# The second expert layer's output product as seven block products, with its gate and value stage run over the tokens in two passes

## The chip, the cores and the metric

The kernel runs on one core of a Trainium2 chip. The metric is the time on the device in microseconds (us), as the median of three runs. Engines are named as the profile names them: PE is TensorE (PEld its weight loads, LDWEIGHTS), DVE is VectorE, ACT is ScalarE, POOL is GpSimd, SP is SyncE, whose queue issues the DMAs.

## The reference, cut to what matters

```python
x = attention(q, k, v, s)                    # 2304 tokens x 512
x = moe_ref(rms_norm(x), w_gate, w_val, w_out)      # first expert layer
def moe2_ref(x, w_gate, w_val, w_out):       # second expert layer
    g = x @ w_gate                           # 512 -> 1536
    silu = g * (1.0 / (1.0 + np.exp(-g)))
    val = x @ w_val                          # 512 -> 1536
    return silu * val @ w_out                # 1536 -> 512, the product changed here
```

Inputs are float32, the expert weights float64 (8 bytes an element).

## The kernel before

**An order made by a planner.** The program records every operation with its engine, its assumed duration, what it reads and writes, and a priority (`op`, L95). `Plan.run` (L130) then makes a list schedule: at each step the engine that is free first takes the ready operation with the smallest priority number. The result is one fixed order for each engine and for SP's DMA queue; on the chip each engine works through its list in that order and waits by semaphores. Operations with several engines in a list (`[(POOL, ...), (DVE, ...)]`) go to the one that is free. The assumed durations (`c_mm`, `c_tt` and the like) are the planner's own numbers and not those of a trace.

**Three matmuls for one.** Every operand of the large products is split in a high part H and a low part L (both fp32r): H by a copy on ACT, L by a subtraction on DVE or POOL. A product is then W_H x_H + W_H x_L + W_L x_H, three matmuls into one PSUM bank, and each of them has its own LDWEIGHTS of 128x128.

**Stages.** Attention and the first gate and value stage (`moe1`, L937) share PE until 537 us. Then follow, with names used below:

1. the first output layer (`out_layer`, L1154, with `out_mm`, L1128): hidden h (1536 rows, 12 blocks f of 128) times `w_o`, for five groups of tokens (`TGROUPS`: four of 512, one of 256). Each block of h is read back from DRAM (`h_d`) into a ring of two buffers, split, and multiplied: 4 output blocks x 3 matmuls for one f.
2. the second gate and value stage: for each of 12 blocks f of the weights `w2_gv`, `load_w2` (L1177) reads the float64 values, converts them, makes the Strassen sums and splits them; then `pair_unit` (L1256) does 42 matmuls of 512 columns on token groups 0 and 1 together (seven block products instead of eight), `plain_unit` (L1316) 24 matmuls of 256 columns on group 4, and `pair_unit` again 42 on groups 2 and 3. Results go to DRAM (`h2_d`).
3. the second output layer: the same `out_layer` with `w2_o` (loop at L1392), 12 matmuls for each f and group, evacuated by `out_store` (L1137) and written to the output.

```python
for i, (w, x) in enumerate(((0, 0), (0, 1), (1, 0))):     # L1131
    op(PE, c_mm(n), lambda en, ...: en.matmul(
        acc_[d]()[:, :n], Wo[w]()[:, c], HL[x](), ...
```

PSUM is eight banks: four `mo` (shared by whoever comes), `sps0`, `sps1`, `tp0`, `tp1`. SBUF is divided in pools that are opened and closed in turn: `m1` (first gate and value stage) must be closed, when its last user is done, before `m2` can be opened (`swap_m1`, L1093).

Of the kernel before, what the change touches and what calls it, by code (L numbers as in the profile page):

```python
# [69 lines left out]
def whole(x):  # L70
    return x if isinstance(x, Part) else (x, None)


class Plan:
# [16 lines left out]
    def __init__(self):  # L91
        self.ops = []
        self.live = {}

    def op(self, eng, ns, fn, r=(), w=(), pri=0.0, later=0, port=False):  # L95
# [13 lines left out]
        for accesses, writes in ((r, False), (w, True)):  # L109
            for a in accesses:  # L110
                buf, part = a if isinstance(a, tuple) else (a, None)
                key = buf if isinstance(buf, str) else buf.key
                live = self.live.setdefault(key, [])
# [181 lines left out]
def tile_kernel(  # L295
# [729 lines left out]
    def later_buf(pool, tag, shape, dtype, name=None):  # L1025
        b = buf(pool, tag, shape, dtype, name)
        if b.key not in plan.live:
            plan.live[b.key] = list(plan.live[pool])
        return b

    def obuf(tag, shape, dtype, name=None):
        return later_buf("o", tag, shape, dtype, name)

    def m2buf(tag, shape, dtype, name=None):
        return later_buf("m2", tag, shape, dtype, name)

    def claim(*bufs):

        for b in bufs:
            op(NONE, 0, lambda en: None, w=[b])  # L1040

    raws = [obuf(f"cvs{i}", [P, 2 * DM], I32) for i in range(2)]
    cvy_o = obuf("cvy", [P, 512], F32)

    def load_o(src, f, HL, pri):

        H, L = HL
        stage = raws[f % 2]
        sub = [(POOL, c_ptt(DM)), (DVE, c_tt(DM))]
        value = load_raw(src[f * P:(f + 1) * P, :], stage, pri)  # L1050
        op(ACT, c_act(DM) + 35, lambda en: en.activation(H(), value(), ACTF.Copy),
           r=[stage], w=[H], pri=pri)
        op(sub, 0, lambda en: en.tensor_tensor(out=L(), in0=value(), in1=f32(H()),
                                               op=ALU.subtract),
           r=[stage, H], w=[L], pri=pri, port=True)

    def load_raw(src, stage, pri):

        n = src.shape[-1]
        if src.dtype == F32:  # L1060
            op(SP, 4 * P * n, lambda en: en.dma_start(out=stage().bitcast(F32)[:, :n], in_=src),
               w=[stage], pri=pri)
            return lambda: stage().bitcast(F32)[:, :n]

        def value(dtype=F32):
            return stage().bitcast(dtype).rearrange("p (n w) -> p n w", w=2)[:, :, 0]
# [4 lines left out]
            cvy_o().bitcast(F16).rearrange("p (n w) -> p n w", w=2)[:, :, 1],  # L1071
            stage().bitcast(BF16).rearrange("p (n w) -> p n w", w=4)[:, :, 2], ACTF.Copy),
           r=[stage], w=[cvy_o], pri=pri)
        op(DVE, c_tt(n), lambda en: en.scalar_tensor_tensor(  # L1074
            out=value(U32), in0=value(U32), scalar=13, in1=cvy_o().bitcast(U32),
            op0=ALU.logical_shift_right, op1=ALU.bitwise_or), r=[stage, cvy_o], w=[stage],
           pri=pri, port=True)
        return value

    def out_places(f):  # L1080
        return tuple(obuf(f"o{z}{f}", [P, DM], F32R) for z in "HL")

    clear([cvy_o], -900)
    W1o = []
    for f in range(KF):
        W1o.append(out_places(f))
        load_o(w_o, f, W1o[f], P_ATT + 1000 + f)
# [8 lines left out]
    op(NONE, 0, swap_m1, w=m1_keys + ["m2"])  # L1096

    P2 = 1.0e5
    hturn = {}
    hdeep = {"h": ["hh0", "hh1"], "H": ["hH0", "hH1"], "L": ["hL0", "hL1"]}  # L1100
    halves = {}

    def hring(z, dtype, n):

        k = hturn[z] = hturn.get(z, -1) + 1
        tags = hdeep[z]
        if n > 256:
# [28 lines left out]

    def out_store(acc_, n, tiles, pri, dst=None, key=None, any_engine=False):  # L1137
        for d in range(KD):
            xo = tiles[d]
            op([(ACT, c_act(n)), (DVE, c_tt(n))] if any_engine else ACT, c_act(n), {  # L1140
                ACT: lambda en, d=d, xo=xo: en.activation(
                    xo(), acc_[d]()[:, :n], ACTF.Copy, scale=0.5),
                DVE: lambda en, d=d, xo=xo: en.tensor_scalar(
                    out=xo(), in0=acc_[d]()[:, :n], scalar1=0.5, scalar2=None,
                    op0=ALU.mult)}, r=[acc_[d]], w=[xo], pri=pri)
            if dst is not None:
                op(SP, 4 * P * n, lambda en, d=d, xo=xo: en.dma_start(out=dst(d), in_=xo()),
                   r=[xo], w=[(key, d)], pri=pri)

    def banks(odd):  # L1150
        return [mo_bank() for _ in range(4)] if odd else \
            [bank(t) for t in ("sps0", "sps1", "tp0", "tp1")]

    def out_layer(gi, h_dram, key, Wo, pri, odd, by_row=False):  # L1154

        n = TGROUPS[gi][1]
        a = banks(odd)
        for f in range(KF):
            hh = hring("h", F32, n)
            op(SP, 4 * P * n, lambda en, hh=hh, f=f: en.dma_start(out=hh(), in_=h_dram[gi][f]),  # L1160
               r=[(key, f) if by_row else key], w=[hh], pri=pri + f)
            out_mm(a, Wo[f], split_h(hh, n, -1.0e4), f, n, pri + f)
        return a

    NPAIR = 2
    A_ROWS = {"A11": 0, "A12": 1, "A21": 2, "A22": 3, "S1": 4, "S2": 5, "S3": 6, "S4": 7}
    B_ROWS = ("B11", "B21", "B22", "T1", "T2", "T3", "T4")
    sums = m2buf("sf", [P, 1024], F32)  # L1170
    w2_tags = [("w2H", "w2L"), ("x1g0", "x1g1")]
    def wide_buf(tag, shape, dtype, name):
        b = m2buf(tag, shape, dtype, name)
        claim(b)
        return b

    def load_w2(f, pri):  # L1177

        H, L = (wide_buf(w2_tags[f % 2][z], [P, 2048], F32R, f"w2{'HL'[z]}") for z in range(2))
        gate, val = (load_raw(w2_gv[f, :, 512 * z:512 * z + 512], raws[z], pri)  # L1180
                     for z in range(2))
        g1, g2, v1, v2 = (lambda t=t, c=c: t()[:, c:c + 256]
                          for t in (gate, val) for c in (0, 256))

        def S(i):
            return sums()[:, 256 * i:256 * i + 256]
        two = [(POOL, c_ptt(256)), (DVE, c_tt(256))]
        for i, (a, b, sign, r) in enumerate((
                (v1, v2, ALU.add, raws[1:]), (lambda: S(0), g1, ALU.subtract, [(sums, 0), raws[0]]),
                (g1, v1, ALU.subtract, raws), (g2, lambda: S(1), ALU.subtract, [(sums, 1), raws[0]]))):  # L1190
# [252 lines left out]
```

## Time and profile before

| | |
|---|---|
| three runs | 1097.58, 1098.05, 1099.43 us (median 1098.05) |
| the profiled execution's own time | 1097.84 us |
| its span, first to last instruction | 1096.1 us |
| PE busy | 1078.8 us (98%), 6580 matmuls |
| DVE, ACT, POOL busy | 675.9, 583.5, 208.1 us |
| DMA | 131.42 MB, mean 120 GB/s |

The span is what the profiler saw of one execution, 1.74 us less than that execution's own time. Busy time of PE is the time in which at least one matmul was in flight; a matmul of 512 columns lasts 0.39 us from its start to its end but the next one starts 0.23 us after it, so prices of matmuls are distances between starts. Idle time of an engine that is not the bottleneck costs nothing.

### The profile page before, as it was taken

What the parts mean: (1) busy time and instruction counts of PE and PEld (TensorE: products, weight loads), DVE (VectorE), ACT (ScalarE), POOL (GpSimd) and SP (SyncE); (2) the same over time, 40 slices, a digit from 0 to 9 for tenths busy, and PEclk for the clock granted to TensorE, in tenths of its full rate; (3) what the DMA queues carried; (4) which work ended last, traced back from release to release, by engine and by line L of the source; (5) the groups of instructions that cost most, each with busy time, mean ns of one, the idle gap of its engine ahead of it and who ended that gap; (6) DMA issues with size and microseconds to landing.
All of it is one profiled execution on the core that took longest, in us unless ns stands there. A gap on an engine that the chain in (4) does not pass through costs nothing.

```text
span 1096.1 us, 19019 instructions
## 1 busy us (share of the span) xinstructions
PE 1078.8 (98%) x6580; PEld 973.5 (89%) x6580; DVE 675.9 (62%) x1755; ACT 583.5 (53%) x1266; POOL 208.1 (19%) x300
## 2 busy tenths in 40 slices
PE   7899999999999999999999999999999999999998
PEld 5599999999999999999978889888888888888888
DVE  7798788796787766652344437676677566632222
ACT  5877777766775764531244336544554455543222
POOL 4344444423333220210000000121122111000000
PEclk9999999999999999999999999999999999999999
DMA  5974444333332213641233333232232223654342
GB/s 159 301 257 136 112 122 126 117 114 94 98 108 75 80 41 121 182 137 47 70 121 96 99 97 93 91 113 85 101 139 101 88 92 129 210 180 132 99 135 96
DMA packets 81616, 131.42 MB, mean 120 GB/s; under 512 B 12848, under 2 KB 42544, under 8 KB 81520
## 3 DMA queue, kind: packets, MB, share of 16 engines
q1 hardware_dynamic: 81520, 130.20, 37.9%
q8 instruction: 52, 0.85, 0.3%
q14 instruction: 44, 0.36, 0.1%
HBM read 97.05 MB, written 33.10 MB: 119 GB/s over the span
## 4 chain that ended last, share of the span: by engine, by line
PE 84%; DMA 3%; DVE 2%; ACT 1%; issue 1%; POOLq 0%; POOL 0%; ACTq 0%; DVEq 0%; SPq 0%
PE mo L921 23%; PE mo L1132 12%; PE mo L1274 10%; PE sps L1274 8%; PE tp L1132 6%; PE sps L1132 6%; PE tp L708 4%; PE tp L692 4%; PE sps L628 4%; PE mo L1325 3%; DMA cvs<-in_w_o 2%; PE tp L1274 1%; PE mo L828 1%; ACT cvy L1070 1%; DVE cvs L1074 0%
## 5 line engine op out<-in xcount | busy, mean ns | idle before, releaser
L921 PE MATMUL mo<-xH,H 128*128 128x320 f32 (+1 forms) x768 | 228.0, 297 | 0.8 <-DVE x L905 0.8
L921 PE MATMUL mo<-xL,H 128*128 128x320 f32 (+1 forms) x768 | 227.8, 297 | 0.0
L921 PE MATMUL mo<-xH,L 128*128 128x320 f32 (+1 forms) x768 | 227.7, 297 | 0.0
L921 PEld LDWEIGHTS mo<-xH,H 128*128 128x128 f32 x768 | 144.1, 188 | 1.9 <-DVE x L905 1.0
L921 PEld LDWEIGHTS mo<-xL,H 128*128 128x128 f32 x768 | 144.3, 188 | 0.7 <-issue 0.2
L921 PEld LDWEIGHTS mo<-xH,L 128*128 128x128 f32 x768 | 144.3, 188 | 0.4
L665 ACT ACTIVATE sc<-sc,col 128x512 f32<-128x512 f32 (+4 forms) x160 | 96.0, 601 | 64.3 <-DVE col L654 63.7
L1120 DVE TENSOR_TENSOR hL<-hh,hH 128x512 fp32r<-128x512 f32 (+1 forms) x90 | 58.2, 651 | 114.8 <-ACT hH L1117 114.6
L1117 ACT ACTIVATE hH<-hh 128x512 fp32r<-128x512 f32 (+1 forms) x90 | 52.5, 587 | 114.9 <-PE mo L1132 55.9
L928 ACT ACTIVATE t<-mo 128x256 f32<-128x256 f32 (+1 forms) x108 | 43.1, 399 | 58.5 <-PE mo L921 57.9
L930 DVE SCALAR_TENSOR_TENSOR t<-t,mo 128x256 f32<-128x256 f32 (+1 forms) x108 | 48.1, 445 | 40.4 <-ACT t L928 39.4
L692 PE MATMUL tp<-ident,sc 128*128 128x128 f32 x432 | 65.5, 276 | 0.0
L700 DVE TENSOR_TENSOR pTB<-tp,pTB 128x512 fp32r<-128x512 f32 (+1 forms) x96 | 54.4, 575 | 14.5 <-ACT pTB L697 12.4
L933 DVE TENSOR_TENSOR hh<-t,mo 128x256 f32<-128x256 f32 (+1 forms) x108 | 48.0, 445 | 18.9 <-PE mo L921 18.0
L1280 ACT ACTIVATE u<-sps 128x512 f32<-128x512 f32 x48 | 28.7, 598 | 54.1 <-PE sps L1274 54.0
L1132 PE MATMUL mo<-hL,oH 128*128 128x512 f32 (+1 forms) x144 | 54.4, 378 | 0.0
L628 PE MATMUL sps<-kHH,qst 128*128 128x288 f32 (+4 forms) x160 | 54.2, 346 | 0.0
L1132 PE MATMUL mo<-hH,oH 128*128 128x512 f32 (+1 forms) x144 | 54.0, 377 | 0.0
L1132 PE MATMUL mo<-hH,oL 128*128 128x512 f32 (+1 forms) x144 | 53.8, 377 | 0.0
L1289 ACT ACTIVATE u<-u 128x512 f32<-128x512 f32 x48 | 29.7, 633 | 43.7 <-DVE u L1284 43.7
L654 DVE CUSTOM_DVE_ANT_0 sc<-sps,cb 128x384 f32<-128x384 f32 (+3 forms) x112 | 48.9, 443 | 6.4 <-PE sps L628 5.3
L697 ACT ACTIVATE pTB<-tp 128x512 fp32r<-128x512 f32 (+1 forms) x96 | 47.0, 502 | 10.9 <-PE tp L692 5.9
(221 smaller groups left out, 2795.3 us busy)
## 6 DMA issues: line engine op xcount, KB each, us to landing
hh<-h_d SPq DMA_DIRECT2D x72, 256.0 KB, 2.6
cvs<-in_w_gv SPq DMA_DIRECT2D x28, 511.8 KB, 4.6
h_d<-u SPq DMA_DIRECT2D x48, 256.0 KB, 2.0
cvs<-in_w_o SPq DMA_DIRECT2D x24, 511.8 KB, 4.0
h_d<-hh SPq DMA_DIRECT2D x84, 128.0 KB, 1.9
raw<-in_w_gv SPq DMA_DIRECT2D x20, 511.8 KB, 5.7
lq<-in_qk SPq DMA_DIRECT2D x32, 288.0 KB, 3.6
cb<-cum_d SPq DMA_DIRECT2D x32, 288.0 KB, 3.5
```

The costliest lines, as they stand in the source:

```text
L628: op(PE, c_mm(n), lambda en, pt=pt, o=o, c=c, n=n, z=z, kk=kk: en.matmul(pt()[:, :n], qst[j]()[:, o:o + 128], kk()[:, c:c + n], start=z == ...
L654: op(DVE, c_tt(w), lambda en: en.tensor_tensor_reduce(out=sc()[:m, c:c + w], in0=pt()[:m, c - at:c - at + w], in1=bias()[:m, c + off:c + o ...
L665: op(ACT, c_act(o + m, 2) + 35, lambda en: en.activation(sc()[:m, :o + m], sc()[:m, :o + m], ACTF.Exp, scale=-1.0, bias=col()[:m, 0, t:t + 1],
L692: op(PE, C_TR, lambda en, pt=pt, a=a, m=m, kb=kb, t=t: en.transpose(pt()[:, a:a + P], self.sc[t]()[:, kb * P:kb * P + P], ident()), r=[sel ...
L700: op(DVE, c_tt(n), lambda en, pt=pt, a=a, d0=d0, n=n, kn=kn: en.tensor_tensor(out=L()[:kn, d0:d0 + n], in0=pt()[:kn, a:a + n], in1=f32(H() ...
L921: op(PE, c_mm(n), lambda en, a=a, x=x, c=c, k=k, i=i: en.matmul(ps()[:, :n], a()[:, c], x()[:, k, :n], start=(k == 0 and i == 0), stop=(k ...
L930: op(DVE, c_tt(n), lambda en: en.scalar_tensor_tensor(out=t()[:, :n], in0=t()[:, :n], scalar=1.0, in1=gp()[:, :n], op0=ALU.add, op1=ALU.mu ...
L933: op(DVE, c_tt(n), lambda en: en.tensor_tensor(out=hh()[:, :n], in0=t()[:, :n], in1=vp_()[:, :n], op=ALU.mult), r=[vp_, t], w=[hh], pri=pri)
L1117: op(ACT, c_act(n) + 35, lambda en: en.activation(H(), src(), ACTF.Copy), r=[src], w=[H], pri=pri)
L1120: lambda en: en.tensor_tensor(out=L(), in0=src(), in1=f32(H()), op=ALU.subtract),
L1132: op(PE, c_mm(n), lambda en, d=d, c=c, w=w, x=x, i=i: en.matmul(acc_[d]()[:, :n], Wo[w]()[:, c], HL[x](), start=(f == 0 and i == 0), stop= ...
L1274: op(PE, c_mm(n), lambda en, w=w, xx=xx, cut=cut, kk=kk, i=i: en.matmul(ps()[:, :n], W[w]()[:, cut], xx(), start=first and kk == 0 and i == 0,
```

## The change

The second output layer is written as Strassen's scheme in Winograd's form with seven products instead of eight: the weight matrix is cut in blocks A11, A12, A21, A22 of 768x256, the tokens of a group in two halves, and sums of blocks S1 to S4 are multiplied instead. A matmul then has half the columns: 256 for the four groups of 512 tokens, 128 for the group of 256. One product is 2 output blocks m x 6 blocks kk x 3 matmuls; a group takes 7 x 36 = 252.

The rest makes room and order for that. All large SBUF tiles come from two lists of slots: 36 of kind D (two rows of 512 for H and L) and 31 of kind S (one row of 512); `mem` takes the slot that has been free longest, `give` returns it. `store_w2` and `store_wo` convert the float64 weights early, form the sums once and write them to DRAM as float32 (`w2_d`, `wo_d`); `reload_w2` and `fetch_wo` read and split them. The gate and value stage runs over the tokens twice (pass 1: groups 0 and 1; pass 2: groups 2, 3 and 4), and reads and splits `w2_d` in each pass. `first_rows` and `other_rows` read h2 and make the sums of its blocks. In the first output layer four buffers (`ahead`) are taken from pool `o`; the rest, and the weights of f = 6 to 11, need slots of `m2`.

The core of the diff (the accessors for parts of tiles, `Both`, `block`, `side`, and changes of the kind obuf to `single()` are left out):

```diff
+    lows = [single() for _ in range(2)]
+    def load_value(src, out, pri, y=lows[0]):
...
+        stage = mem("D", [P, 2 * n], I32)
...
+        give(stage)
...
+    def store_w2(f, pri):
+        V, _ = values(w2_gv[f, :, :512], w2_gv[f, :, 512:], ("A11", "A12", "A21", "A22"), pri)
+        for i in range(4):
+            X = block(V[i], (0, 1), 0, 512)
+            op(SP, 4 * P * 512, lambda en, i=i, X=X: en.dma_start(
+                out=w2_d[f, :, 512 * i:512 * i + 512], in_=X()), r=[X], w=[("w2_d", (f, i))],
+               pri=pri + 1)
+        give(*V)
+    EARLY = 6
+    W1o = [load_o(w_o, f, P_ATT + 1000 + f) for f in range(EARLY)]
+    ahead = [(pair(), single()) for _ in range(4)]
+    for f in range(KF):
+        store_w2(f, 1.0e5 + 30 + 25 * f)
+    for kk in range(KH):
+        store_wo(w2_o, wo_d, "wo_d", kk, 1.0e5 + 330 + 20 * kk)
...
+    slots("D", "w", [f"{z}{f}" for f in range(KF) for z in "HL"])
+    slots("S", "m2", [f"s{i}" for i in range(20)], "m2")
+    W1o += [load_o(w_o, f, P2 - 20 + f) for f in range(EARLY, KF)]
...
+    def reload_w2(f, pri):
+        out = []
+        for i in range(4):
+            b, t = pair(), single()
+            H, L = side(b, 0), side(b, 1)
+            dma(t, w2_d[f, :, 512 * i:512 * i + 512], 512, [("w2_d", (f, i))], pri)
+            split(t, H, L, 512, pri)
+            give(t)
+            out.append((H, L))
+        return out
...
+    def first_rows(h, key, p, at):
...
+            rows(h, key, kk, p, whole, pri)
+            combine(T[1], T[1], T[0], n, ALU.subtract, pri)
+            split(whole, side(b, 0, 0, 2, n), side(b, 1, 0, 2, n), 2 * n, pri)
...
+    def other_rows(h, key, p, at):
...
+            rows(h, key, kk + KH, p, other, pri)
+            rows(h, key, kk, p, whole, pri)
+            b21, b22 = V
+            combine(T[1], b22, T[1], n, ALU.subtract, pri)
+            combine(T[0], T[1], T[0], n, ALU.add, pri)
+            split(whole, *B, 2 * n, pri)
+            split(other, *C, 2 * n, pri)
+            combine(b21, b21, T[0], n, ALU.subtract, pri)
+            split(b21, *Ds, n, pri)
...
+    def strassen_out(h, key, W, pri, sink, G1, others):
...
+            def product(ps, a, G, i2, first, n=n):
+                for m in range(2):
+                    for kk in range(KH):
+                        HL = G[kk][1][i2]
+                        for i, (w, z) in enumerate(((0, 0), (0, 1), (1, 0))):
...
+            product(b, "A11", G1, 0, True)
+            product(c, "S1", G1, 1, True)
+            product(b, "S2", G2, 0, False)
+            product(b, "S3", G2, 1, False)
+            product(c, "S4", G3, 1, False)
+            product(c, "A12", G3, 0, True)
+            product(b, "A22", G4, 0, False)
...
     for f in range(KF):
         if f + 1 < KF:
-            W2.append(load_w2(f + 1, P3 + 40 * f - 20))
-        pair_unit(f, W2[f], X2[0], (0, 1), P3 + 40 * f)
-        plain_unit(f, W2[f], rest, 2 * NPAIR, 256, P3 + 40 * f + 10)
-        pair_unit(f, W2[f], X2[1], (2, 3), P3 + 40 * f + 20)
+            W2.append(reload_w2(f + 1, P3 + 20 * f - 10))
...
+        pair_unit(f, W2[f], X2, (0, 1), P3 + 20 * f)
+        give(*[HL[0] for HL in W2[f]])
...
+    for f in range(KF):
+        if f + 1 < KF:
+            W2.append(reload_w2(f + 1, P4 + 40 * f - 20))
...
+        pair_unit(f, W2[KF + f], X3, (2, 3), P4 + 40 * f)
+        plain_unit(f, W2[KF + f], rest, 4, 256, P4 + 40 * f + 20)
...
-    for gi, (t0, n) in enumerate(TGROUPS):
-        a = out_layer(gi, h2_d, f"h2_d{gi}", W2o, P4 + 100 * gi, gi % 2 == 0, True)
...
+    G1 = first_rows(h2_d, "h2_d", 0, P5 - 50)
+    others = other_rows(h2_d, "h2_d", 0, P5 - 45)
+    for kk in range(KH):
+        for i in (4, 6):
+            W2o[kk].update(fetch_wo(wo_d, "wo_d", kk, i, P5 - 30 + i))
+    strassen_out(h2_d, "h2_d", W2o, P5, store, G1, others)
```

**Where the order moves.** First place: PE's list for the last group of tokens (256 of them) in the second output layer. A name is the tile with its buffer number; the form at the end is the output's. Before, from the middle of the group:

```order
L1132 MATMUL mo0_11977<-hH0_11944,oH_10835 128x256
L1132 MATMUL mo0_11977<-hL0_11949,oH_10835 128x256
L1132 MATMUL mo0_11977<-hH0_11944,oL_10842 128x256
L1132 MATMUL mo2_11985<-hH0_11944,oH_10835 128x256
L1132 MATMUL mo2_11985<-hL0_11949,oH_10835 128x256
L1132 MATMUL mo2_11985<-hH0_11944,oL_10842 128x256
```

And with the change, the first of its fourteen runs of 18 matmuls (x3 is the three matmuls of one block kk, which read one tile for H and L):

```order
L1460 MATMUL mo1_13426<-H9_13126,H8_10221 128x128 x3
L1460 MATMUL mo1_13426<-L9_13131,H11_10312 128x128 x3
L1460 MATMUL mo1_13426<-H10_13137,d6_10432 128x128 x3
L1460 MATMUL mo1_13426<-L10_13143,H7_10527 128x128 x3
L1460 MATMUL mo1_13426<-d1_13151,L4_10808 128x128 x3
L1460 MATMUL mo1_13426<-d3_13163,H6_10863 128x128 x3
```

The group goes from 144 matmuls of 256 columns to 252 of 128, and the four groups of 512 tokens from 576 of 512 to 1008 of 256; all other matmuls keep their number and form.

Second place: DVE's list with the change at the seam between `moe1` and the first output layer. `hh1` is the last hidden block of `moe1`; L1112 converts float64 values, of `w_o` where it reads `L0` to `L2`; `H6_7826` is the L part of h's block f = 4, the first that does not lie in an `ahead` buffer:

```order
L949 TENSOR_TENSOR hh1_7727<-t1_7707,mo0_7703 128x320
...
L1112 SCALAR_TENSOR_TENSOR s0_7784<-L0_7291,s1_6358 128x512
L1124 TENSOR_TENSOR H0_7792<-s0_7784,H0_7792 128x512
L1112 SCALAR_TENSOR_TENSOR s1_7806<-L1_7333,s1_6358 128x512
L1112 SCALAR_TENSOR_TENSOR s4_7813<-d11_7762,s0_6352 128x512
L1129 TENSOR_TENSOR s5_7823<-s4_7813 128x256
L1124 TENSOR_TENSOR H1_7816<-s1_7806,H1_7816 128x512
L1112 SCALAR_TENSOR_TENSOR s2_7830<-L2_7374,s1_6358 128x512
L1124 TENSOR_TENSOR H6_7826<-s6_7787,H6_7826 128x512
```

Eight operations on DVE (from `s0_7784`, the first slot of `m2` that is written) now stand between the closing of `m1` and the first h block that needs it; before, both h's ring and all of `w_o` lay in pool `o`, and nothing here waited for `m1`.

Third place: DVE's list with the change at the seam between pass 2 and the second output layer. The first row is the last evacuation of pass 2 (it reads `sps0_11474`, the bank of the last matmuls); L1129 makes sums of h2's blocks, L1124 the L parts; `L1_11790` and `d2_11808` are the last two tiles that the third product, S2, reads:

```order
L1328 TENSOR_TENSOR s4_11643<-s4_11643,sps0_11474 128x512
L1129 TENSOR_TENSOR s2_11398<-s2_11398,s17_11270 128x256
L1129 TENSOR_TENSOR s5_11428<-s5_11428,s12_11453 128x256
L1129 TENSOR_TENSOR s9_11390<-s9_11390,s8_11349 128x256
...
L1129 TENSOR_TENSOR s2_11596<-s2_11596 128x256
L1124 TENSOR_TENSOR L1_11790<-s9_11588,L1_11790 128x512
L1124 TENSOR_TENSOR s10_11803<-s13_11544,s10_11803 128x256
L1124 TENSOR_TENSOR d2_11808<-s2_11596,d2_11808 128x512
```

From the row behind the evacuation to `d2_11808` it is fourteen operations, twelve of 256 columns and two of 512; PE has the products A11 and S1 (72 matmuls) and the first five blocks of S2 (15) to do meanwhile. Before, nothing but the split of single h2 blocks stood there.

## Rows read from the trace of the kernel before

**Rows 1.** The page: busy time by engine, and the granted clock in 40 slices.

```profile
PE 1078.8 (98%) x6580; PEld 973.5 (89%) x6580; DVE 675.9 (62%) x1755; ACT 583.5 (53%) x1266; POOL 208.1 (19%) x300
...
PEclk9999999999999999999999999999999999999999
```

**Rows 2.** Stretches: us, then busy us (instructions) of PE, PEld, DVE, ACT, POOL; clock, DMA share, GB/s.

```profile
466.00:560.00 94.00, 93.00 (x626) 88.75 (x627) 37.88 (x78) 23.88 (x47) 3.79 (x3) 1.00 0.30 94
560.00:663.00 103.00, 103.00 (x456) 85.14 (x455) 43.47 (x68) 40.97 (x73) 0.00 (x0) 1.00 0.33 98
663.00:957.00 294.00, 294.00 (x1500) 251.80 (x1498) 197.81 (x307) 153.86 (x273) 46.94 (x42) 1.00 0.33 113
957.00:1075.00 118.00, 117.87 (x518) 96.71 (x517) 34.93 (x52) 39.95 (x66) 0.00 (x0) 1.00 0.42 133
```

**Rows 3.** The chain that ended last, 1000 to 1097 us: start us, us, what.

```profile
1010.01 32.64 PE mo L1132 x144
...
1075.29 16.21 PE mo L1132 x135
1091.52 1.50 DVE oo L1143 x4
```

**Rows 4.** PE's timeline, two matmuls of 128 columns between longer ones: start us, us, what.

```profile
253.91 0.22 PE L628 MATMUL sps<-kHH,qst 128*128 128x128 f32 x1
253.97 0.27 PE L628 MATMUL sps<-kLL,qst 128*128 128x128 f32 x1
254.08 0.36 PE L921 MATMUL mo<-xL,H 128*128 128x320 f32 x1
```

**Rows 5.** PEld's timeline, the weight loads at the same place.

```profile
253.91 0.19 PEld L628 LDWEIGHTS sps<-kLL,qst 128*128 128x128 f32 x1
254.02 0.19 PEld L921 LDWEIGHTS mo<-xL,H 128*128 128x128 f32 x1
254.13 0.19 PEld L921 LDWEIGHTS mo<-xH,L 128*128 128x128 f32 x1
```

**Rows 6.** PE's timeline, longer runs of short matmuls (128 and 2 columns).

```profile
419.76 0.93 PE L692 MATMUL tp<-ident,sc 128*128 128x128 f32 x7
...
430.60 1.39 PE L828 MATMUL mo<-half,sq 128*128 128x2 f32 x12
```

**Rows 7.** Groups by shape, 690 to 950 us, and DVE's timeline at 545 us.

```profile
L1201 POOL TENSOR_TENSOR w2L<-cvs,w2H 128x512 fp32r<-128x512 f32 x10 | 13.2, 1317 | 103.1 <-ACT w2H L1198 103.1
L1201 DVE TENSOR_TENSOR w2L<-sf,w2H 128x512 fp32r<-128x512 f32 x11 | 17.2, 1575 | 0.0
...
L1191 DVE TENSOR_TENSOR sf<-cvs 128x256 f32<-128x256 f32 x8 | 3.4, 425 | 0.3
...
545.65 1.29 DVE L1201 TENSOR_TENSOR w2L<-sf,w2H 128x512 fp32r<-128x512 f32 x2
```

**Rows 8.** ACT's group by shape, 1042 to 1097 us.

```profile
L1117 ACT ACTIVATE hH<-hh 128x512 fp32r<-128x512 f32 x5 | 3.2, 630 | 8.4 <-PE tp L1132 8.4
```

**Rows 9.** Timelines of PE, DVE and SP where `moe1` ends.

```profile
537.27 0.40 PE L1132 MATMUL sps<-hH,oL 128*128 128x512 f32 x1
...
537.47 0.49 DVE L933 TENSOR_TENSOR hh<-t,mo 128x320 f32<-128x320 f32 x1 [0.80 <-PE mo L921]
...
537.98 0.80 SPq L953 DMA_DIRECT2D h_d<-hh  x2
```

**Rows 10.** The page: DMA in all, and issues with KB each and us to landing.

```profile
DMA packets 81616, 131.42 MB, mean 120 GB/s; under 512 B 12848, under 2 KB 42544, under 8 KB 81520
...
hh<-h_d SPq DMA_DIRECT2D x72, 256.0 KB, 2.6
...
h_d<-hh SPq DMA_DIRECT2D x84, 128.0 KB, 1.9
```

**Rows 11.** Timelines of PE and SP at the end.

```profile
1092.28 0.28 PE L1132 MATMUL mo<-hH,o 128*128 128x256 f32 x1
...
1091.98 1.80 SPq L1147 DMA_DIRECT2D out_dram<-oo  x4
```

More of the change, by code (lines that the diff above doesn't have):

```diff
@@ L1042, in tile_kernel @@
[L1042 to L1055, printed above, removed]
@@ L1057, in load_raw, with slots, mem @@
-    def load_raw(src, stage, pri):
+    free = {"D": [], "S": []}
+    tick, made = [0], [0]
+    def slots(kind, pool, tags, start=None):
+        for t in tags:
+            ops = plan.live[start] if start else plan.live.pop(f"{pool}.{t}")
+            free[kind].append((0, len(free[kind]), pool, t, [m for _, m, _ in ops]))
+            plan.gone.add(f"{pool}.{t}")
+    def mem(kind, shape, dtype=F32):
+        free[kind].sort(key=lambda s: s[:2])
+        assert free[kind], kind
+        _, i, pool, tag, ops = free[kind].pop(0)
+        made[0] += 1
+        key = f"mem{made[0]}"
+        plan.live[key] = [(None, m, True) for m in ops]
+        b = Buf(key, lambda: pools[pool][1].tile(shape, dtype, name=tag, tag=tag))
+        b.slot = kind, i, pool, tag
+        return b
@@ new lines, in give, with single, block @@
+    def give(*bufs):
+        for b in dict.fromkeys(b[0] if isinstance(b, Part) else b for b in bufs):
+            kind, i, pool, tag = b.slot
+            tick[0] += 1
+            free[kind].append((tick[0], i, pool, tag,
+                               sorted({m for _, m, _ in plan.live.pop(b.key)})))
+            plan.gone.add(b.key)
+    def single(n=512):
+        return mem("S", [P, 512], F32)
+    def block(b, labels, lo, n, z=None):
+        if z is None:
+            return Both(b, labels, lambda t: t[:, lo:lo + n])
+        return Both(b, labels, lambda t: t[:, z, lo:lo + n])
@@ new lines, in tile_kernel, with dma, out_layer @@
+    give(lows[1])
+    def dma(out, src, n, r, pri):
+        op(SP, 4 * P * n, lambda en: en.dma_start(out=out(), in_=src), r=r, w=[out], pri=pri)
+    def out_layer(gi, h_dram, key, Wo, pri, odd, last=False):
+        n = TGROUPS[gi][1]
+        a = [mo_bank() for _ in range(4)] if odd else \
+            [bank(t) for t in ("sps0", "sps1", "tp0", "tp1")]
+        for f in range(KF):
+            b, t = ahead.pop(0) if ahead else (pair(), single())
+            H, L, X = side(b, 0, n=n), side(b, 1, n=n), block(t, (0,), 0, n)
+            dma(X, h_dram[gi][f], n, [key], pri + f)
+            split(X, H, L, n, -1.0e4, any_engine=False)
+            give(t)
+            for d in range(KD):
+                c = slice(d * P, (d + 1) * P)
+                for i, (w, x) in enumerate(((0, H), (0, L), (1, H))):
+                    op(PE, c_mm(n), lambda en, d=d, c=c, w=w, x=x, i=i, f=f: en.matmul(
+                        a[d]()[:, :n], Wo[f][w]()[:, c], x(), start=(f == 0 and i == 0),
+                        stop=(f == KF - 1 and i == 2)), r=[Wo[f][w], x],
+                       w=[a[d]] if f or d or i else [*a, "claim"], pri=pri + f)
+            give(b)
+            if last:
+                give(Wo[f][0])
+        return a
```

503 lines of the change are left out of this document (274 added, 229 removed).

## The prediction

> **What bounds the kernel now.** I read the page first, for who is busy and at what clock. PE has a matmul in flight in 1078.8 of 1096.1 us, and the granted clock reads 9 in every slice [rows 1], so every price of a matmul below is taken at the full one of the two clock levels, 2.4 GHz. Then the busy times stretch by stretch: from 560 to 957 us PE has no idle time at all, and from 957 to 1075 us, where the changed product runs, 0.13 us, while DVE works a third of that time, 34.93 of 118 us [rows 2]. PE bounds each stage there, and the time of a stage is its number of matmuls by their distance. Last the chain of waits: it ends with 144 matmuls of 512 columns in 32.64 us (one of the four large groups), then 135 of 256 columns in 16.21 us, then four evacuations on DVE in 1.50 us [rows 3]. So a matmul of 512 columns costs 32.64/144 = 0.2267 us, one of 256 costs 16.21/135 = 0.1201 us.
>
> **What the change does to PE.** Only the second output layer's matmuls change. It loses 576 of 512 columns (576 x 0.2267 = 130.6 us) and 144 of 256 (144 x 0.1201 = 17.3), 147.9 us in all. It gains 7 products x 2 x 6 x 3 = 252 for each group: 1008 of 256 columns (1008 x 0.1201 = 121.1) and, for the last group, 252 of 128. Per large group that is 252 x 0.1201 = 30.3 in place of 32.64, a gain of 2.4, or 9.5 for four.
>
> The price of a 128-column matmul in a long run is the term that decides, for no such run is in the trace. Nearest is a place where two of them stand between longer ones: they start 0.06 apart, the next matmul 0.11 behind, though the second ends 0.11 later than the first (253.97 + 0.27 against 253.91 + 0.22) [rows 4], and the weight loads there start 0.11 apart throughout [rows 5]. Seven of 128 columns in a row take 0.93 us, of which the last lasts some 0.27: (0.93 - 0.27)/6 = 0.11. Twelve with only 2 columns take 1.39 us, about 0.11 each [rows 6]: with almost no columns to stream the distance does not fall, so what is left is the weight load, which every matmul here has. I take 0.11: 252 x 0.11 = 27.7 us. Ends: the mean of the two gaps, (0.06 + 0.11)/2 = 0.085 or 21.4 us, and 0.1201, no faster than 256 columns, or 30.3 us. So halving the columns of the last group saves almost nothing per matmul while their number grows by three quarters: +10.4 us. PE in all: 121.1 + 27.7 - 147.9 = **+0.9 us** (ends -5.4 and +3.5).
>
> **What lies beside PE.** The sums and splits of h2 are new work: with the order's counts a large group has 36 operations of 256 columns and 18 of 512 on DVE. The rows give 1.50/4 = 0.375 for the one [rows 3] and 1.29/2 = 0.645 for the other [rows 7]: 13.5 + 11.6 = 25.1 us beside 30.3 of PE. ACT has about 18 of 512 at 0.63 [rows 8] and a few smaller ones, some 18 us. In pass 1 DVE's eleven operations of 512 columns, 7.1 us, lie beside 42 x 0.2267 = 9.5 of PE. The float64 conversions and Strassen sums of both weights move ahead to `moe1`'s end and the first output layer, some 55 us of DVE and POOL; from 466 to 663 us DVE is free for 56.1 + 59.5 = 115.6 us [rows 2]. All of this costs nothing as long as PE covers it.
>
> **Three new waits.** They stand where PE passes from one stage to the next, because the 36 and 31 slots are exactly full there.
>
> First seam, `moe1` to the first output layer. Before, nothing of that layer waited for pool `m1`. Now the fifth block of h and the weights from f = 6 lie in `m2`. With the order, 43 matmuls follow `moe1`'s last: 43 x 0.2267 = 9.7 us of cover, from 537.27 on. `m1` closes when its last hidden block has left SBUF: DVE ends it at 537.96, the two stores are issued until 538.78 [rows 9] and land 1.9 later [rows 10], 540.7, or 3.4 us into the cover. Behind it stand eight DVE operations, 7 x 0.645 + 0.375 = 4.9 us, and the load of h, 2.6 us [rows 10], beside them or ahead of them: the block is there after 8.3 to 10.9 us. Margin +1.4 to -1.2.
>
> Second seam, pass 2 to the Strassen product. The last of its first six blocks goes to the slot that pass 2's last matmul reads. Its H part is needed 15 matmuls later (1.8 us; ACT takes 0.63 [rows 8]), its L part 32 later (3.8 us) after 0.63 and a split on POOL, 1.32 [rows 7]. Margin 1.2 to 1.9.
>
> Third seam, the third product S2, whose last blocks need fourteen DVE operations behind pass 2's last evacuation, 12 x 0.375 + 2 x 0.645 = 5.8 us, against 87 matmuls x 0.1201 = 10.4. While POOL splits, an operation of DVE takes 1.575 in place of about 0.65 [rows 7], and five POOL splits stand around this seam: up to 4.6 more. Margin 4.6 to 0.
>
> What stays open is POOL and the queue: SP issues 40% more (about 187 MB by the shapes of the new loads and stores, against 131.42 [rows 10]), in one order, and a store that waits for DVE holds the loads behind it. Each seam therefore lies between 0 and a late load, 2.6. I take half a POOL split at each, 0.65, since that is the size by which the margins miss: **+1.95 us**. That more DMA costs nothing in between: a mean of 187 MB in 1096 us is 171 GB/s, which by the 133 GB/s at a share of 0.42 [rows 2] is a share of 0.54.
>
> **The end.** Before, the last matmul starts at 1092.28 and lasts 0.28; four evacuations and four stores follow, whose issue alone takes 1.80 us [rows 11]. Now the last product's second half leaves one 128-column bank and one store of 64 KB. I take 0.3 us less, between 0 and the 1.1 that three of the four evacuations take: **-0.3 us**.
>
> **The sum.** The profiled execution's own time is 1097.84 us, 0.21 under the median shown. 1097.84 + 0.9 + 1.95 - 0.3 = 1100.4, on the median's footing 1100.6; rounded, **1100.5 us**. About 0.2%, 2.2 us, is what a measurement of this kernel tells from no change: faster is under 1095.85, slower over 1100.25. The likeliest case's own range, waits from 0 to 1.3 each and 128 columns from 0.11 to 0.12, is 1098.6 to 1105.
>
> **Rivals.**
>
> *Faster: the short matmuls stream at two for one weight-load time.* If the 0.06 gap of [rows 4] alternates with 0.11 in a long run, one costs 0.085 and the last group 21.4 us: 1100.5 - 6.3 = 1094.2. It decides below 23.1/252 = 0.092 us (4.65 us under the forecast). For it speaks the 0.06 itself; against it that the ends and the weight loads keep 0.11 [rows 4, 5], and both longer runs [rows 6]. Chance 0.16. The Trainium skill's page "TensorE: Matmul & The Clock Gate" (Back-to-back issue gap) states this outcome: a sustained stream of weight load and matmul at 128 columns runs at about 81 ns each. As an estimate from that page the last group would take 252 x 0.081 = 20.4 us and the kernel 1093.2. The same sentence states 131 ns for 512 columns, which this case's chain contradicts with 0.2267 us [rows 3], so I do not lean on it; the page's other rule (LDWEIGHTS), a weight load's columns over 1.2, or 107 ns for 128, agrees with the 0.11 of [rows 5].
>
> *No change: the covers hold.* Every margin above is positive at its favourable end. Without the waits 1100.5 - 1.95 = 1098.6. It decides at waits of under 1.6 us in all. For it speaks that PE shows no idle time across the old seams [rows 2]; against it that those had two spare buffers and these none. Chance 0.35.
>
> *Slower still: DVE bounds the Strassen groups.* Its 54 operations leave 30.3 - 25.1 = 5.2 us per group; 0.096 us more for each uses that up. The mean of one alone is 0.425 for 256 columns [rows 7], 0.05 over the paced 0.375, and with three or four POOL splits per group each adding 0.93 (1.575 - 0.645) a group stands at 25.1 + 2.7 + 3.7 = 31.5, 1.2 over PE. With a wait at each product's turn that is 1 to 2 us a group, 4 to 8 in all: 1105 to 1108. Against it: DVE works ahead by whole blocks, and its load before was a third. Chance 0.10.
>
> **How the numbers follow.** The forecast's case has the rest, 0.39. Faster 0.16; same 0.35; slower 0.39 + 0.10 = 0.49. The range reaches from a little below the faster rival (which with no waits would be 1092.2) to the middle of the DVE rival: **1093.0 to 1106.0**. It leaves out half of that rival, half of what lies under 1094 and what I have not thought of, together about 0.15.
>
> **What would show it.** In the profile after: the chain should end with 252 matmuls of 128 columns in about 27.7 us (21.4 or less, and the faster rival holds), preceded by large groups of 30.3. At the three seams PE's waits should name DVE, POOL or a load, under 2.6 us each; a gap of more, or gaps inside pass 1 or pass 2, would mean that the slots or SP's queue hold the loads. DVE's share in a large group should be near 25 of 30 us; 30 or more with PE waiting on it at every product is the DVE rival. The forecast is wrong at its root if a 256-column matmul in the seven products costs other than 0.120 us, or if the stages ahead of them change their length by more than the waits named.

## The result, and the profile after

The changed kernel takes 1110.2 us (median of four runs, 1109.12 to 1111.8), the kernel before 1097.95 beside it: a ratio of 1.011, 95% interval 1.0093 to 1.0128. It is slower by 12.2 us; 2.5 had been forecast, and the time lies above the range. The profiled execution is the slowest of the four, 1111.8 us.

First the page: busy times, and what the DMA engines did in the 40 slices (27.75 us each; share in tenths, then GB/s).

```profile
PE 1084.6 (98%) x7120; PEld 1000.2 (90%) x7120; DVE 778.9 (70%) x2021; ACT 637.3 (57%) x1420; POOL 240.1 (22%) x325
...
DMA  5974444433332305889988752555555636686520
GB/s 166 284 250 142 111 120 129 120 112 91 102 111 64 89 30 187 270 286 319 285 289 283 253 169 69 154 171 162 161 181 176 193 111 185 196 283 196 157 77 20
...
DMA packets 119068, 187.40 MB, mean 169 GB/s; under 512 B 17008, under 2 KB 58224, under 8 KB 118960
```

The bytes are the forecast 187 MB, and their mean, 169 GB/s, is the one that the prediction went by, but they don't come as a mean: from 444 to 638 us, seven slices in a row stand at 253 to 319 GB/s. That is where most of the float64 weights of the second layer are converted early.

The same stretches as in [rows 2], and two shorter ones:

```profile
466.00:560.00 94.00, 85.72 (x569) 81.15 (x568) 51.12 (x102) 31.70 (x61) 8.07 (x11) 0.96 0.93 300
560.00:663.00 103.00, 102.48 (x452) 84.27 (x451) 61.23 (x110) 47.08 (x80) 0.00 (x0) 1.00 0.78 247
...
480.00:510.00 30.00, 27.36 (x201) 26.23 (x199) 15.45 (x35) 8.02 (x16) 3.72 (x5) 1.00 0.91 293
...
540.00:570.00 30.00, 24.36 (x96) 19.58 (x95) 24.31 (x41) 18.89 (x33) 1.43 (x2) 0.89 0.97 311
```

From 466 to 560 us the DMA share is 0.93 at 300 GB/s, where it was 0.30 at 94, and PE has a matmul in flight for 85.72 us, where it had 93.00. The granted clock, 1.00 there before, is 0.96, and 0.89 around the seam.

Now the stage that the change is about, in the chain of waits (start us, us, what): the first large group, and the last group of tokens.

```profile
958.04 30.23 PE mo L1460 x252
...
1078.99 28.11 PE mo L1460 x252
```

30.23/252 = 0.120 us and 28.11/252 = 0.1115 us, as forecast from [rows 3] and [rows 4 to 6]; PE does not stop from 957.8 to the end.

To add it up, I took for every matmul from 430 us on the distance to the next one's start, less the price of its width. These excesses sum to 3.2 us before and 15.1 after: 0 against 3.8 from 480 to 520 us, 0.7 against 8.6 from 540 to 560, 0 against 1.1 from 640 to 660, and 0.9 before where the old second output layer began. With PE's own term (149.2 - 147.9 = +1.3), the end (-0.6) and a start of attention that is 1.5 us later in this execution (0.4 and 1.8 us in narrow and plain_last below, whose order is the same up to there) this gives 11.9 + 1.3 - 0.6 + 1.5 = 14.1, against 1111.8 - 1097.84 = 14.0. Of the 11.9 us, 3.8 lie at the end of `moe1` and 7.9 at the first seam.

**The end of `moe1`.** One of its gaps in the chain of waits (pieces of under 0.1 us left out), and all of PE's waits there for the same line, from 480 to 510 us (us in total, times, longest):

```profile
476.97 5.72 DMA d<-in_w_gv
...
482.78 0.80 ACT s L1108
483.60 0.69 DVE s L1112
484.29 0.34 DVE t L946
...
484.68 5.93 PE mo L937 x48
```

```profile
PE mo L937 <- DVE t L946: 2.6, 4, 1.1
```

PE waits for `moe1`'s own operation on DVE (L946), which frees a PSUM bank. That one stands in DVE's list behind a conversion (L1112), which waits for ACT (L1108), which waits for a raw load of 5.72 us.

**The seam.** The chain there (pieces of under 0.1 us left out), then SP's queue and PE at the same place:

```profile
534.67 4.83 DMA d<-in_w_gv
...
539.58 0.80 ACT s L1108
540.40 0.70 DVE s L1112
541.12 0.32 SPq L1177
...
541.53 4.54 DMA d<-in_w_gv
...
546.15 0.80 ACT s L1108
546.97 0.70 DVE s L1112
547.69 0.32 SPq L1177
...
548.06 4.68 DMA s<-h_d
552.76 0.64 ACT H L1121
```

```profile
541.12 0.32 SPq L1177 DMA_DIRECT2D w_d<-s  x1
541.53 0.38 SPq L1105 DMA_DIRECT2D d<-in_w_gv  x1
542.96 0.32 SPq L1177 DMA_DIRECT2D w_d<-s  x1
543.34 0.95 SPq L969 DMA_DIRECT2D h_d<-hh  x2
544.39 0.39 SPq L1177 DMA_DIRECT2D w_d<-s  x1
544.87 0.45 SPq L1105 DMA_DIRECT2D d<-in_w_gv  x1
547.69 0.32 SPq L1177 DMA_DIRECT2D w_d<-s  x1
548.06 7.07 SPq L1208 DMA_DIRECT2D s<-h_d  x12
```

```profile
546.29 1.52 PE L1224 MATMUL tp<-d,d 128*128 128x512 f32 x6
553.45 1.22 PE L1224 MATMUL sps<-H,d 128*128 128x512 f32 x2 [5.64 <-ACT H L1121]
554.47 1.05 PE L1224 MATMUL tp<-H,d 128*128 128x512 f32 x2
```

Read the chain upwards. PE waits 5.64 us for the H part of h's fifth block; its load was issued at 548.06, because SP's queue stood before it at the store of a converted W2 block (L1177), which waited for the conversion on DVE (L1112), which waited for a raw load of 4.54 us, which itself had stood in that queue behind the store of the conversion before it (541.12). It was not the closing of `m1` that held the load: the stores of `moe1`'s last hidden block (L969), issued from 543.34 on, landed 4.9 and 4.7 us after their issue, the first at 548.26, when the load had been issued already. `moe1`'s last hidden block was held in the same way: its last matmul started at 537.72, but DVE stood before a conversion until 540.40 and ended the block only at 542.07. When PE goes on, two matmuls of 512 columns start 0.43 us apart in place of 0.227: the granted clock from 553 to 559 us is 0.50, the lower level of 1.2 GHz. That lasts 13 matmuls, the first of them 0.60 us before the next: 12 x 0.20 + 0.37 = 2.8 us more.

### The profile page after: what moved, and what is told of

It reads as the page before. It is cut to its first block, busy times and chain, and to the rows that moved or that the text cites. A ratio compares the mean times of both kernels' runs of the same rounds, so it can differ in the third digit from the quotient of the medians.

```text
span 1110.0 us, 21121 instructions
## 1 busy us (share of the span) xinstructions
PE 1084.6 (98%) x7120; PEld 1000.2 (90%) x7120; DVE 778.9 (70%) x2021; ACT 637.3 (57%) x1420; POOL 240.1 (22%) x325
## 4 chain that ended last, share of the span: by engine, by line
PE 46%; DMA 7%; DVE 2%; ACT 1%; issue 1%; SPq 1%; POOL 0%; DVEq 0%; ACTq 0%; POOLq 0%
PE mo L1312 10%; PE sps L1312 9%; PE mo L1460 8%; PE mo L1224 4%; PE sps L1460 3%; PE mo L1360 3%; DMA d<-in_w_gv 3%; PE tp L1460 2%; PE sps L1224 2%; DMA d<-in_w_o 2%; PE tp L1224 2%; PE tp L1312 1%; DMA h_d<-hh 1%; ACT s L1108 1%; DVE s L1112 1%
## 5 line engine op out<-in xcount | busy, mean ns | idle before, releaser
L1121 ACT ACTIVATE L<-s 128x512 fp32r<-128x512 f32 (+1 forms) x114 | 67.7, 602 | 66.2 <-PE mo L1224 26.0
L1129 DVE TENSOR_TENSOR s<-s,s 128x256 f32<-128x256 f32 (+2 forms) x149 | 73.0, 503 | 30.3 <-ACT s L1294 19.4
L1124 DVE TENSOR_TENSOR L<-s,L 128x512 fp32r<-128x512 f32 (+1 forms) x103 | 68.0, 668 | 34.0 <-ACT L L1121 33.5
L1124 DVE TENSOR_TENSOR d<-s,d 128x512 fp32r<-128x512 f32 (+1 forms) x98 | 68.6, 710 | 28.9 <-ACT d L1121 24.2
L1108 ACT ACTIVATE s<-d 128x512 f16<-128x512 bf16 x42 | 33.3, 792 | 87.1 <-DMA d<-in_w_gv 56.5
L1121 ACT ACTIVATE d<-s 128x512 fp32r<-128x512 f32 (+1 forms) x118 | 68.9, 600 | 16.6 <-PE mo L1360 4.2
L1294 ACT ACTIVATE s<-mo 128x512 f32<-128x512 f32 (+2 forms) x78 | 38.9, 500 | 66.2 <-PE mo L1460 33.7
L1129 POOL TENSOR_TENSOR s<-s,s 128x256 f32<-128x256 f32 (+1 forms) x15 | 14.4, 960 | 268.2 <-ACT s L1294 217.4
L1112 DVE SCALAR_TENSOR_TENSOR s<-d,s 128x512 uint32<-128x512 uint32 x42 | 29.0, 690 | 49.9 <-ACT s L1108 39.9
L1294 ACT ACTIVATE s<-sps 128x512 f32<-128x512 f32 (+1 forms) x64 | 34.4, 538 | 41.7 <-PE sps L1312 27.8
L1124 POOL TENSOR_TENSOR d<-s,d 128x512 fp32r<-128x512 f32 x20 | 29.2, 1461 | 121.5 <-ACT d L1121 119.7
L1124 DVE TENSOR_TENSOR H<-s,H 128x512 fp32r<-128x512 f32 (+1 forms) x64 | 42.3, 666 | 18.0 <-ACT H L1121 17.8
```

What stands on the lines that cost most here:

```text
L1108: op(ACT, c_act(n) + 165, lambda en: en.activation(y().bitcast(F16).rearrange("p (n w) -> p n w", w=2)[:, :n, 1], stage().bitcast(BF16).re ...
L1121: op(ACT, c_act(n) + 35, lambda en: en.activation(H(), f32(X()), ACTF.Copy), r=[X], w=[H], pri=pri)
L1124: lambda en: en.tensor_tensor(out=L(), in0=f32(X()), in1=f32(H()), op=ALU.subtract),
L1129: lambda en: en.tensor_tensor(out=out(), in0=f32(a()), in1=f32(b()), op=alu),
L1294: op(ACT, c_act(n), lambda en: en.activation(dst(), ps()[:, :n], ACTF.Copy, scale=scale), r=[ps], w=[dst], pri=-1.0e4)
```

## The experiments

Each is the changed kernel with one edit; rate290_plain, conv120_plain, conv150_plain and conv120_plain_ahead5 have two or three together, and before_rate290 is the kernel before with one. Times are medians, and the ratio is to the kernel before on the same chip (1098.5 to 1099.2; 1097.95 beside the changed kernel, so differences of a microsecond between medians say little). A gap "from start to start" is the distance of two matmuls' starts, 6.02 us at the seam of the changed kernel; a number in brackets at a line is the idle time, 5.64 there.

| | us | ratio to before, 95% |
|---|---|---|
| late4 | 1123.6 | 1.0219 (1.0191 to 1.0246) |
| narrow | 1102.3 | 1.0028 (1.0017 to 1.0039) |
| plain_last | 1101.0 | 1.0022 (1.0005 to 1.0038) |
| rate290 | 1100.8 | 1.0015 (1.0004 to 1.0027) |
| before_rate290 | 1097.5 | 0.9987 (0.9976 to 0.9998) |
| rate290_plain | 1092.3 | 0.9934 (0.9915 to 0.9952) |
| conv120_plain | 1091.2 | 0.9920 (0.9905 to 0.9935) |
| ahead5 | 1106.8 | 1.0062 (1.0046 to 1.0077) |
| conv120_plain_ahead5 | 1088.2 | 0.9902 (0.9881 to 0.9922) |
| conv150_plain | 1093.9 | 0.9953 (0.9940 to 0.9966) |

**Fewer bytes in the same order** (narrow):

```diff
-                out=w2_d[f, :, 512 * i:512 * i + 512], in_=X()), r=[X], w=[("w2_d", (f, i))],
+                out=w2_d[f, :, 512 * i:512 * i + 128], in_=X()[:, :128]), r=[X], w=[("w2_d", (f, i))],
...
-            dma(t, w2_d[f, :, 512 * i:512 * i + 512], 512, [("w2_d", (f, i))], pri)
+            dma(t, h_d[i][f], 512, [("w2_d", (f, i)), f"h_d{i}"], pri)
```

> The changed kernel with the same order on every engine, but each store of w2_d moves 128 of its 512 columns (64 KB in place of 256), and the reloads read blocks of h from DRAM in place of w2_d, so W2 in the product is left out. Some 9 MB of 36 go from the stretch 445 to 575 us. Theory (bandwidth): with fewer bytes the raw loads land in about 4.5 us in place of 5.6, the gap at the seam falls below 3 us; 1103 to 1106. Rival (the order of SP and DVE alone: each raw load waits for the conversion before it, whatever the bandwidth): the gap stays at 5 us or more; 1109 to 1110.

1102.3 us, 7.9 less, a little under the expected range. PE's idle time at the seam is 1.55 us (1.94 from start to start), the slow matmuls behind it are gone, and the gaps at the end of `moe1` too. Windows, PE and issues (the median us to landing) of this kernel:

```profile
480.00:510.00 30.00, 30.00 (x223) 30.00 (x222) 14.77 (x33) 8.12 (x16) 3.02 (x4) 1.00 0.83 249
510.00:540.00 30.00, 30.00 (x188) 28.63 (x187) 16.84 (x32) 8.88 (x16) 2.91 (x4) 1.00 0.75 231
```

```profile
543.67 0.73 PE L1224 MATMUL sps<-H,d 128*128 128x512 f32 x2 [1.55 <-ACT H L1121]
```

```profile
d<-in_w_gv SPq DMA_DIRECT2D x17, 511.8 KB, 4.9
...
h_d<-hh SPq DMA_DIRECT2D x23, 128.0 KB, 4.1
```

Beside it the same stretch, 460 to 560 us, of the changed kernel:

```profile
d<-in_w_gv SPq DMA_DIRECT2D x18, 511.8 KB, 5.6
s<-h_d SPq DMA_DIRECT2D x14, 256.0 KB, 5.3
h_d<-hh SPq DMA_DIRECT2D x24, 128.0 KB, 4.8
```

and of the kernel before:

```profile
h_d<-hh SPq DMA_DIRECT2D x24, 128.0 KB, 1.8
hh<-h_d SPq DMA_DIRECT2D x8, 256.0 KB, 2.7
cvs<-in_w_gv SPq DMA_DIRECT2D x4, 511.8 KB, 4.5
```

With the order of every engine left alone, the bytes of the stores decide over most of the loss. In the median a raw load lands 0.7 us sooner (4.9 against 5.6). How that adds up from link to link is not shown, but the end of the chain is: h's load is issued 6.9 us after `moe1`'s last matmul starts (538.94 - 532.01) in place of 10.3 (548.06 - 537.72), and it lands 2.6 us later in place of 4.7.

**The conversions moved behind the seam** (late4; the last argument is what a raw load must wait for):

```diff
-    for f in range(KF):
+    for f in range(4):
         store_w2(f, 1.0e5 + 30 + 25 * f)
-    for kk in range(KH):
-        store_wo(w2_o, wo_d, "wo_d", kk, 1.0e5 + 330 + 20 * kk)
...
     slots("S", "m2", [f"s{i}" for i in range(20)], "m2")
...
+    for f in range(4, KF):
+        store_w2(f, 1.0e5 + 30 + 25 * f, ["m2"])
...
+    op(NONE, 0, lambda en: None, r=[x1[3][0]], w=["pass1"])
+    for kk in range(KH):
+        store_wo(w2_o, wo_d, "wo_d", kk, P3 + 40 * kk + 5, ["pass1"])
```

> The changed kernel, but only the first four of the twelve W2 conversions (two 512 KB raw loads and four 256 KB stores each) may run before moe1 ends; the other eight wait for the opening of pool m2, and those of w2_o for the end of the fourth group of the first output layer. Theory (the early conversions fill the DMA engines, share 0.90 to 0.97 from 450 to 570 us, so that loads and stores land after 4.4 to 5.6 us in place of 1.9 to 2.6, and the DVE and SP queues stand behind them): PE's gaps from 480 to 510 us (3.4 us over the pace) and at 547 us (6.0 us, and 13 matmuls at 0.43 in place of 0.227 behind it) go; 1110.2 - 10.5 = about 1100, if the bytes do not stall the first output layer instead. Rival (slots: the fifth block of h must wait for pool m2 at all, whoever uses the DMA queue): the gap at the seam stays at 4 us or more, 1106 or more.

1123.6 us where about 1100 had been expected: slower still, yet it tells the two apart. Both places are clean now (480 to 510 and 540 to 570 us), although h's fifth block lies in pool `m2` as it did; the slots by themselves were not the cause. The stall has moved, with the bytes, to the start of pass 1:

```profile
480.00:510.00 30.00, 30.00 (x228) 30.00 (x227) 9.53 (x22) 4.84 (x11) 0.74 (x1) 1.00 0.50 145
...
540.00:570.00 30.00, 30.00 (x134) 24.86 (x133) 26.42 (x46) 22.74 (x40) 0.00 (x0) 1.00 0.89 306
...
683.00:710.00 27.00, 24.28 (x103) 18.40 (x102) 20.37 (x34) 15.48 (x30) 5.94 (x5) 1.00 0.87 283
710.00:740.00 30.00, 16.49 (x54) 12.45 (x53) 15.60 (x27) 10.49 (x18) 1.87 (x3) 0.72 0.71 232
```

There the stores and raw loads of w2_o mix with the reloads of W2 and the stores of h2 in one queue (`s<-w_d` took 6.47 us from 696.50, `d<-in_w_o` 5.21 from 708.70), and PE stood once for 11.66 us:

```profile
715.42 1.58 PE L1314 MATMUL mo<-H,d 128*128 128x512 f32 x3 [1.85 <-ACT s L1296]
...
729.95 1.65 PE L1314 MATMUL tp<-L,d 128*128 128x512 f32 x3 [11.66 <-DVE s L1320]
```

**A slower DMA in the planner's book** (rate290):

```diff
-    RATE = 350.0
+    RATE = 290.0
```

> The changed kernel, made with a planner that is told 290 bytes per ns for a DMA in place of 350 (the traffic that the trace shows between 450 and 570 us); nothing else. The order then spreads the conversions a little: 20 in place of 22 W2 raw loads lie ahead of the seam, and 23 loads of h stand ahead of the next store. Theory (h's loads are late behind the conversions): the gap at 547 us at least halves, 1103 to 1107. Rival (slots of pool m2): the gap stays, 1109 to 1111.

1100.8 us, faster than the expected 1103 to 1107: the gap at the seam is 1.0 us from start to start, `moe1` has none. Since the constant touches every DMA of the program, the kernel before was made with it too:

> The kernel before, made with the planner's rate of 290 in place of 350. Theory (the rate helps by taking the early conversions' pressure off the DMA engines, and the kernel before moves 94 GB/s there): no change beyond 2 us, 1096 to 1100. Rival (the rate makes a better order of attention and the first gate and value stage for any kernel, by the 3.5 us that moe1 ends sooner in the changed kernel made with it): 1093 to 1095.

1097.5 us against 1099.2 beside it, a gain of 0.13% whose interval (0.02 to 0.24%) only just leaves out zero. If the rate does as much elsewhere in the changed kernel, some 1.5 of the 9.4 us, at most 2.6, come from a better order there, and the rest from the spread of the conversions; conv120_plain below tests that directly.

**The last 256 tokens without Strassen** (plain_last; the core of the edit):

```diff
-        for p, (_, n) in enumerate(OUT_PAIRS):
+        for p, (_, n) in enumerate(OUT_PAIRS[:-1]):
...
+        for i in range(2):
+            for m in range(2):
+                for f in range(KF):
+                    ww2 = W[f % KH][f"A{i + 1}{f // KH + 1}"]
+                    for j, (w, z) in enumerate(((0, 0), (0, 1), (1, 0))):
...
+                        op(PE, c_mm(256), lambda en, ...: en.matmul(
+                            a[d]()[:, :256], ww()[:, m * P:m * P + P], x(), ...
```

> The changed kernel with Strassen's products for the four groups of 512 tokens only; the last 256 tokens are done with eight plain block products, 144 matmuls of 256 columns in place of 252 of 128, for which A21 is stored and loaded too (six stores and six loads of 128 KB more). By the prices read (0.1115 against 0.120 us): 28.1 - 17.3 = 10.8 us less, the end about 0.5 longer: 1100. Rival (the short matmuls were not the price, the end is bound by loads or by DVE): less than 6 us gained, with gaps between the last group's matmuls.

1101.0 us, 9.2 less. The chain ends as priced:

```profile
1081.62 17.29 PE mo L1537 x144
```

17.29 in place of 28.11 us is 10.8; some of it went to a wait that the second large group has in this kernel (PE 1.4 us for DVE's L1470).

**Both edits together** (rate290_plain), **and the plain last group with slower DMAs in the plan for the conversions alone** (conv120_plain, whose second edit is this; the first line is the raw load of float64 values):

```diff
-        op(SP, 8 * P * n, lambda en: en.dma_start(
+        op(SP, 1.2 * 8 * P * n, lambda en: en.dma_start(
...
-            op(SP, 4 * P * 512, lambda en, i=i, X=X: en.dma_start(
+            op(SP, 1.2 * 4 * P * 512, lambda en, i=i, X=X: en.dma_start(
```

> Both edits together: the planner told 290 bytes per ns, and the last 256 tokens by eight plain products. If the two gains are independent (1110.2 to 1100.8 for the one, to 1101.0 for the other), 1100.8 - 9.2 to 10.8 = 1090 to 1092, faster than the kernel before by 0.6% or more. Rival (the gains share a cause, a stretch of the chip's day or the seam): 1097 or more.

> The changed kernel with the plain last group, where the planner counts 1.2 times the bytes for the raw loads of the float64 weights from w_o on and for the stores of w2_d alone, and keeps 350 bytes per ns for the rest. Theory (it is the early conversions that must be spread): the gap at the seam falls below 2 us, 1090 to 1094. Rival (the rate of every DMA in the plan matters, the order of attention too): 1096 to 1101.

1092.3 and 1091.2 us: the gains add up, and the one from the plan does not need the rate of every DMA, only that of the conversions. The gap at the seam is 1.6 us from start to start in conv120_plain, as expected.

**One buffer more ahead of the seam** (ahead5, and the same on conv120_plain):

```diff
-    EARLY = 6
+    EARLY = 5
...
-    ahead = [(pair(), single()) for _ in range(4)]
+    ahead = [(pair(), single()) for _ in range(5)]
```

> The changed kernel with five buffers of h ahead of pool m2 in place of four (the sixth early block of w_o gives up its slot and is loaded behind the seam). 12 matmuls more of cover, 2.7 us. If the wait at the seam is only a matter of how long h's block takes through pool m2 and the queues as they stand: gap 6.0 - 2.7 = 3.3 us, and with a shorter idle time the 13 slow matmuls (2.6 us) may go too: 1105 to 1108. If the queue, which is full, only lets the conversions go on longer: 1109 or more.

```profile
550.90 1.22 PE L1224 MATMUL sps<-H,H 128*128 128x512 f32 x2 [2.90 <-ACT H L1121]
551.91 1.91 PE L1224 MATMUL tp<-H,H 128*128 128x512 f32 x4
```

1106.8 us; the gap is 3.3 us from start to start, as worked out, but the clock falls all the same: two matmuls 0.43 us apart.

> conv120_plain with the fifth buffer of h ahead of pool m2 (12 matmuls, 2.7 us, more cover). There 1.6 us of gap are left at the seam, in ahead5 the fifth buffer took 2.7 us off the gap: the gap goes, 1089 to 1090. Rival (the slot that it takes from the early conversions holds those up, and the wait stands elsewhere): 1091 or more.

1088.2 us, the lowest median here, 1.0% (0.8 to 1.2) under the kernel before; its interval overlaps that of conv120_plain. The gap at the seam is gone; 2 us stand near 657 us instead, late in the first output layer.

> As conv120_plain, but the planner counts 1.5 times the bytes of the conversions' DMAs: more of them fall behind the seam, and those of w2_o reach to the start of pass 1. Theory (the bytes must go somewhere before pass 1 ends its first blocks; moved too late they stall pass 1, as with late4): the gap at the seam is gone, gaps of 2 us or more stand in pass 1 or the last groups of the first output layer; 1090 to 1096. Rival (the later the better): 1089 or less.

With 1.5 in place of 1.2, 1093.9 us. In pass 1 there is the gap of 2.2 us (at 689 us) that was expected, but the seam keeps 1.5 us from start to start, which was not: counting still more bytes gains nothing there and costs 2.7 us against conv120_plain.

## Why the prediction was wrong

**What held.** The 128-column price: 0.11 forecast, 0.1115 measured, so the last group rose as worked out (27.7 against 28.11 us), and so did PE's whole term: +0.9 forecast, 149.2 - 147.9 = +1.3. The faster rival, with 0.085 us, is refuted. Its companion from the Trainium skill's page "TensorE: Matmul & The Clock Gate" (Back-to-back issue gap), 81 ns at 128 columns in a sustained stream, disagrees with this case's 0.1115 us; the Trainium skill's rule on weight loads on the same page (LDWEIGHTS), by which 128 columns take 107 ns as an estimate, is near it. DVE in the large groups: 25.1 of 30.3 us forecast, 83%; measured 101.40 of 121.20 us, 84%, and PE did not wait, so the DVE rival is out as well:

```profile
957.80:1079.00 121.20, 121.20 (x1012) 121.16 (x1011) 101.40 (x229) 65.11 (x149) 16.19 (x14) 1.00 0.58 181
```

The end became 0.6 us shorter, 0.3 forecast. The rival of no change, with waits of under 1.6 us in all, fails with the forecast: the first seam alone took more.

**The step that failed** is the one on the conversions and the DMA. "That more DMA costs nothing in between: a mean of 187 MB in 1096 us is 171 GB/s" took a mean over stages, the very thing that the prediction had not allowed itself for PE. The moved bytes lie in some 200 us. The conversions were costed by DVE's free time alone ("DVE is free for 56.1 + 59.5 = 115.6 us"); their raw loads and stores were counted in the sum of bytes and in no stretch. At the 300 GB/s there a 128 KB store landed after 4.8 us in place of 1.8 and a 256 KB load after 5.3 in place of 2.7, and the engines' share stood at 0.97 with 311 GB/s around the seam. The Trainium skill's page "DMA: Bandwidth & Descriptors" (Specifications) puts HBM's limit for one core at about 358 GB/s, half of a stack's. No run here shows that limit: this kernel runs on one core, and slices of 2.5 us between 460 and 560 us read up to 402 GB/s. The prediction had named the sign itself: wrong at its root "if the stages ahead of them change their length by more than the waits named".

**The mis-sized terms.** The first seam: "between 0 and a late load, 2.6", taken at 0.65; measured 8.6 us of excess, 5.8 for the wait, 2.8 for the clock behind it, which had no term. H of h's fifth block was there 15.5 us after the cover began (553.40 - 537.87), not 8.3 to 10.9. I had named what did it (a store that waits for DVE holds the loads behind it), but priced one load from a row of an idle queue, and not the link raw load, ACT, DVE, store (4.5 + 0.8 + 0.7 + 0.3 = 6.3 us), of which SP's queue had two ahead of h. The close of `m1`, with which the forecast's sum began, was not what the load waited for. The other two seams cost nothing (0.65 each forecast). And the end of `moe1`, 3.8 us, had no term: I looked at waits only where PE passes from one stage to the next, and not at the old stage, whose stores (`h_d`) and whose work on ACT and DVE now share in-order queues with the conversions.

Shown by experiment: that the bytes decide over most of it (narrow), that the place of the conversions decides where PE stalls (late4), that the slots of `m2` alone don't make the loss (late4), that it is the plan for the conversions alone whose change takes 9.8 us back (plain_last to conv120_plain), the price of the short matmuls (plain_last), and that cover at the seam counts one for one (ahead5: 12 matmuls, 2.7 us). Still open: how the 1 us or more that is left at the seam in rate290 and conv120_plain divides between bandwidth and the order of SP's queue; no run had fewer bytes and another order. The wait for DVE in the second large group, 0.9 to 1.6 us, in most of the variants and not in the changed kernel itself, was not traced to its cause.

## What to carry to other kernels

When a change moves loads and stores, add up their bytes in the stretch that they move to, beside what flows there already, and take the price of a transfer from a row at such a load; a mean over the kernel hides a full queue. Where a conversion is a chain of load, two engines and store through two slots, each link is paid in every in-order queue that it passes, so ask of each queue what stands behind a link. And halving the columns of a matmul pays only down to the width at which its weight load is the longer one: here 256 columns cost 0.120 us, 128 cost 0.1115, and 2 still cost about 0.11 [rows 6].

## What the runs showed of the hardware

An idle PE of 2.90 us (ahead5), of 5.64 us (the changed kernel) and of 11.66 us (late4) is followed by 13 or 14 matmuls of 512 columns some 0.43 us apart, the 1.2 GHz level (granted clock 0.50 from 553 to 559 us in the changed kernel), and then by 0.23 again; after 1.55 us (narrow) they are 0.23 to 0.37 apart from the first on. The length of the last wait does not tell it alone: in late4 one of 1.85 us, with two shorter ones in the 13 us before it, was followed by matmuls 0.43 us apart too (the line at 715.42), and in conv150_plain one of 1.78 us was not. So a wait can cost some 2.8 us more than the gap that it shows, after 2.90 us as after 11.66.
